# One pool of eight PSUM banks, the second part of batch 0 masked on VectorE, another order of the loads, and new instruction lists, in a fused attention and channel-mix kernel

## The chip, the cores and the metric

The kernel runs on one core of a Trainium2 chip. The metric is the device time in microseconds (us) of one execution. The five engines of the core work side by side, each in the order of its own instruction stream: TensorE (PE in the profile, with its weight loads listed apart as PEld), VectorE (DVE), ScalarE (ACT), GpSimd (POOL) and SyncE (SP). Here POOL issues the loads, SP the stores and the transposing DMAs.

## What is computed

Sliding-window attention with an ALiBi bias over 8 batches, 8 heads, 576 positions and a head dimension of 64; its output, regrouped to rows of 512, goes through an RWKV channel mix.

```python
scores = scale * np.matmul(q, k.transpose(0, 1, 3, 2))
bias = slopes[:, None, None] * (-np.abs(rel).astype(np.float32))[None, :, :]
mask = (rel >= 0) & (rel < window)            # window = 128
scores = np.where(mask, scores + bias[None], -1000000000.0)
attn = softmax(scores);  x = regroup(attn @ v)
...
xk = mu_k * x + (1.0 - mu_k) * x_prev         # x_prev: x one row earlier
xr = mu_r * x + (1.0 - mu_r) * x_prev
k = np.maximum(xk @ w_k, 0.0)
v = k * k @ w_v
return (1.0 / (1.0 + np.exp(-(xr @ w_r))) * v)
```

## The kernel before

**Tiles.** The 576 rows of a batch are four blocks of 128 and a tail of 64. Heads go in pairs, four groups `g` per batch. Since the window is 128, a query block meets its own key block and the one before. The scores of a group are computed in two halves, keys on the partitions, queries along the free dimension.

**Attention, batch by batch.** q and k are loaded with the sequence on the partitions (`cb`) and have to be transposed to `qk` (head dimension on the partitions). For batch 0, in two parts, PE transposes staged blocks (L1123, L1126, L1078); for batches 1 and 2 PE does it in quarters of 64 by 64 (L1078), for 3 and 4 in halves (L837), with copies out by ScalarE and VectorE (L696); for 5 to 7 (`XB`) SP issues transposing DMAs (`flip`, L535). The 64-row tails of q and k (`ts`) become `tt`: batch 0 by matmuls with parts of the identity (L939), batches 1 to 3 by PE transposes (L912), the rest (`XTT`) by a transposing DMA (L628). Then follow the score matmuls (L726), exp on ScalarE (L740) into `at`, and the matmuls with v and a column of ones (L781), which give output and row sum; VectorE takes the reciprocal (L787) and multiplies (L793) into `xu`. `xu` is transposed to `xt` (L820, L837, or by DMA, L902); VectorE forms the difference with the previous row (L880) and `xk` and `xr` (L887).

**Bias and mask.** In batch 0 PE first writes the ALiBi distance times the slope into the PSUM banks of the scores (L713: `sid` holds scaled identities, `dist` the distances), the score matmuls accumulate on it, and exp gives the finished weights. In the other batches exp runs on the bare scores, and VectorE multiplies with `mask`, the exp of the bias (L753). ScalarE makes `mask` from `dist` in eight activations (L1165), gated behind the last `xk` of batch 0's first part, and VectorE copies it to the other columns (L1191).

**Channel mix**, in chunks of 256, 384 or 512 rows (`channel_mix`): per chunk eight groups of four matmuls with `wk` (L983), ReLU on ScalarE (L990), the square on VectorE or ScalarE (L964, L962) into `kk`; then per 128 rows four matmuls with `wr` (L1001) and tanh (L1008), eight with `wv` (L1017) in two halves, and the product (L1022) to `ot`, which SP stores (L1047).

**Order.** The program builds a graph of nodes (`op`, `dma`). `Plan.run` is a planner: it walks the graph with estimated durations and gives every node its buffers (`Hold`). For PE, ACT and DVE the order is not the planner's choice but a table, `ORDER`: each list holds node numbers, and an engine takes the next of its list only. The planner's durations therefore decide the buffer numbers and the place of the DMAs. 90 small matmuls on a zero tile (`NWARM`, L687) are spread at the start.

**PSUM.** Eight banks of 512 floats: `duo0` and `duo1` are tiles of two banks for scores and the attention output of a whole group, `uno0` to `uno3` tiles of one bank for all else. The framework makes the waits from the tiles that instructions share.

**Loads.** POOL issues them in a fixed order, each only after the eighth before it has landed. For the start the string `LOADS` gives it, a letter for a step: `v` two blocks of v, `2` the second part of q and k of batch 0, `K` and `k` the halves of `wk`, `t` the tail of batch 0, `V` the rest of v, `a`, `b`, `c` q and k, tails, and v of batch 1, `R` all of `wr`, `W` and `w` the halves of `wv`.

Of the kernel before, what the change touches and what calls it, by code (L numbers as in the profile page):

```python
# [38 lines left out]
""".split()],  # L39
    "ACT": [int(x) for x in """  # L40
# [11 lines left out]
""".split()],  # L52
    "DVE": [int(x) for x in """
# [25 lines left out]
class Node:  # L79
    def __init__(self, seq, engs, dur, lat, prio, emit, need, free):  # L80
        self.seq, self.engs, self.dur, self.lat = seq, engs, dur, lat
        self.prio, self.emit, self.need, self.free = prio, emit, need, free
        self.left, self.succ = 0, []
        self.ready, self.t0, self.eng, self.queue = 0.0, None, None, None
        self.rows, self.lazy, self.flip = (128, 128), False, False


class Plan:
# [3 lines left out]
    SWITCH = 0.095  # L92
    CROSS = (0.45, 1.1)
# [67 lines left out]
    def run(self):  # L161
# [16 lines left out]
        while events:  # L178
# [11 lines left out]
            while again:  # L190
                again = False
                for e, cand in avail.items():
# [23 lines left out]
                    if e == "PE":  # L216
                        if n.rows[0] != rows:
                            n.dur = dur = dur + self.SWITCH
                        rows = n.rows[1]
                    busy[e] = now + dur  # L220
# [16 lines left out]
        return order  # L237


@with_exitstack  # L240
def kernel(
# [32 lines left out]
    XB = range(5, B)  # L274
    XO = range(5, B)
    X0 = 16
    NWARM = 90
    LOADS = 'v2KtVkabRWwc'
# [8 lines left out]
    QUAD = 0.040  # L287
# [86 lines left out]
    def one(h):  # L374
        return uno[h.idx if h.cls == "p1" else N1 + h.idx]

# [951 lines left out]
```

## Time and profile before

| what | us |
|---|---|
| median of 3 runs | 229.64 |
| lowest and highest run | 228.93 and 230.03 |
| span of the profiled execution | 228.6 |
| PE busy, fillers included | 222.9 |
| DVE busy | 189.2 |
| ACT busy | 156.3 |

The profiled execution's own time is known as its span only; it lies 1.0 us below the median and 0.3 below the lowest run. A busy PE is one with at least one matmul under way, and a matmul's row lasts from its start until its result is written, so that rows of neighbouring matmuls overlap: a matmul's price is the step from its start to the next one's. In the names the number of a buffer is left out. The loads run in one queue, in the order of their issue.

### The profile page before, as it was taken

How to read it: one execution, taken by the hardware profiler on the slowest of the kernel's cores; microseconds unless marked ns; L12 is line 12 of the kernel's file. 1: busy time of each engine (PE TensorE's matmuls, PEld its weight loads, DVE VectorE, ACT ScalarE, POOL GpSimd, SP SyncE). 2: the span in 40 equal slices, each digit the busy share in tenths (PEclk: the TensorE clock that was granted, in tenths of full speed). 3: DMA queues.
4: the chain of work that ended last, by engine and by line, in shares of the span. 5: the costliest groups of instructions: out<-in, count | busy, mean ns of one | idle time of the engine just before them, and what ended most of it. 6: DMA issues, size and time to landing. Idle time of an engine off the chain costs nothing.

```text
span 228.6 us, 6467 instructions
## 1 busy us (share of the span) xinstructions
PE 222.9 (97%) x2611; PEld 134.7 (59%) x2611; DVE 189.2 (83%) x423; ACT 156.3 (68%) x283; POOL 92.0 (40%) x118
## 2 busy tenths in 40 slices
PE   8998999999999999999999999999999999999994
PEld 8674866765667665456675654546755645465542
DVE  6788899999949998989899977899799889956332
ACT  2578899899999987998488735764788137336221
POOL 8755746698963980975029904200000000000000
PEclk9999999999999999999999999999999999999999
DMA  6999999999996999999999997994420461121123
GB/s 162 179 185 199 198 192 179 186 193 173 181 154 119 136 178 187 133 129 155 200 205 136 179 169 179 177 182 160 60 76 3 103 191 53 29 93 49 40 97 138
DMA packets 127741, 32.80 MB, mean 143 GB/s; under 512 B 114904, under 2 KB 123360, under 8 KB 127712
## 3 DMA queue, kind: packets, MB, share of 16 engines
q0 software_dynamic: 95728, 16.26, 93.7%
q1 hardware_dynamic: 30240, 15.54, 30.9%
q10 hardware_dynamic: 1744, 0.59, 1.1%
q8 instruction: 20, 0.33, 0.6%
q14 instruction: 9, 0.07, 0.1%
HBM read 33.56 MB, written 9.44 MB: 188 GB/s over the span
## 4 chain that ended last, share of the span: by engine, by line
PE 82%; DMA 10%; DVE 3%; POOL 1%; ACT 1%; issue 1%; DVEq 0%; POOLq 0%
PE uno L983 27%; PE uno L1017 25%; PE uno L1001 13%; PE duo L781 7%; PE duo L726 6%; DMA wk_sb<-in_moe_w_k_dram 5%; DMA qx<-in_q_dram 3%; DMA out_dram<-ot 2%; PE uno L837 2%; PE uno L1078 1%; POOL vs L500 1%; ACT at L740 1%; DVE ot L1022 1%; DVE xu L793 1%; PE uno L781 1%
## 5 line engine op out<-in xcount | busy, mean ns | idle before, releaser
L983 PE MATMUL uno<-xk,wk_sb 128*128 128x256 bf16 (+2 forms) x416 | 71.4, 314 | 1.1 <-DMA wk_sb<-in_moe_w_k_dram 0.9
L740 ACT ACTIVATE at<-duo 128x1024 bf16<-128x1024 f32 (+2 forms) x68 | 65.0, 989 | 10.6 <-PE duo L726 10.2
L1017 PE MATMUL uno<-wv_sb,kk 128*128 128x512 bf16 (+2 forms) x296 | 69.8, 374 | 0.0
L990 ACT ACTIVATE rl<-uno 128x256 bf16<-128x256 f32 (+2 forms) x104 | 46.6, 475 | 33.2 <-PE uno L983 26.1
L983 PEld LDWEIGHTS <-wk_sb 128*128 128x128 bf16 x416 | 38.9, 98 | 25.5 <-DMA wk_sb<-in_moe_w_k_dram 1.1
L1017 PEld LDWEIGHTS <-kk 128*128 128x128 bf16 x296 | 27.1, 98 | 27.8
L500 POOL DMA_DIRECT2D vs<-in_v_dram x32 | 28.4, 897 | 36.8 <-PE duo L781 33.6
L753 DVE TENSOR_TENSOR at<-at,mask 128x1024 bf16<-128x1024 bf16 x56 | 37.0, 684 | 5.7 <-ACT at L740 5.5
L964 DVE TENSOR_TENSOR kk<-rl 128x256 bf16<-128x256 bf16 (+2 forms) x94 | 30.0, 337 | 9.0 <-ACT rl L990 8.4
L1001 PE MATMUL uno<-wr_sb,xr 128*128 128x512 bf16 x144 | 36.4, 379 | 0.0
L1008 ACT ACTIVATE rs<-uno 128x512 bf16<-128x512 f32 x36 | 21.4, 610 | 16.9 <-PE uno L1001 13.6
L1022 DVE SCALAR_TENSOR_TENSOR ot<-rs,uno 128x512 f32<-128x512 bf16 (+2 forms) x37 | 24.4, 667 | 9.9 <-PE uno L1017 3.6
L887 DVE SCALAR_TENSOR_TENSOR xr<-dl,mu_sb,xt 128x576 bf16<-128x576 bf16 (+1 forms) x32 | 24.6, 777 | 0.0
L887 DVE SCALAR_TENSOR_TENSOR xk<-dl,mu_sb,xt 128x576 bf16<-128x576 bf16 (+1 forms) x32 | 24.4, 776 | 0.1
L781 PEld LDWEIGHTS <-at 128*128 128x128 bf16 x576 | 21.1, 97 | 5.0 <-issue 0.7
L793 DVE TENSOR_TENSOR xu<-duo,rc 128x640 bf16<-128x640 f32 x28 | 22.5, 813 | 0.2
L1001 PEld LDWEIGHTS <-xr 128*128 128x128 bf16 x144 | 13.2, 98 | 13.1 <-issue 0.2
L696 ACT COPY qk<-uno 128x512 bf16<-128x512 bf16 (+1 forms) x32 | 16.9, 582 | 3.2 <-PE uno L1126 2.5
L781 PE MATMUL duo<-vs,at 128*128 128x65 bf16 x448 | 18.7, 193 | 0.2
L531 POOL DMA_DIRECT2D cb<-in_k_dram x20 | 17.8, 924 | 2.1 <-DMA vs<-in_v_dram 1.6
L531 POOL DMA_DIRECT2D cb<-in_q_dram x20 | 17.7, 927 | 0.7 <-PE duo L781 0.6
L696 ACT COPY xt<-uno 128x512 bf16<-128x512 bf16 (+3 forms) x24 | 13.1, 567 | 1.7 <-PE uno L837 0.9
(82 smaller groups left out, 202.3 us busy)
## 6 DMA issues: line engine op xcount, KB each, us to landing
out_dram<-ot SPq DMA_DIRECT2D x34, 256.0 KB, 2.6
vs<-in_v_dram POOLq DMA_DIRECT2D x32, 128.0 KB, 6.8
cb<-in_q_dram POOLq DMA_DIRECT2D x20, 128.0 KB, 6.2
cb<-in_k_dram POOLq DMA_DIRECT2D x20, 128.0 KB, 6.7
wk_sb<-in_moe_w_k_dram POOLq DMA_DIRECT2D x2, 512.0 KB, 10.0
cb<-in_q_dram POOLq DMA_DIRECT2D x4, 256.0 KB, 9.7
cb<-in_k_dram POOLq DMA_DIRECT2D x4, 256.0 KB, 8.8
wv_sb<-in_moe_w_v_dram POOLq DMA_DIRECT2D x2, 512.0 KB, 11.4
```

What stands on the lines that cost most here:

```text
L500: return dma(POOL, 256, issue_t(1024), lambda e: nc.gpsimd.dma_start(out=vs_buf[h.idx][:, j, :, 0:D], in_=v[b, :, 128 * j:128 * j + 128].r ...
L531: return [dma(POOL, 256, issue_t(1024), lambda e, r=r: nc.gpsimd.dma_start(out=cb_buf[h.idx][:, i, r], in_=src[:, :, r]), [g], kind="q") f ...
L696: (nc.scalar.copy if e == ACT else nc.vector.tensor_copy)(out=out, in_=in_)
L740: lambda e, ah=ah, w=w, hp=hp: nc.scalar.activation(out=ah(), in_=two(hp)[:, :, 0:w], func=AF.Exp, scale=float(scale)), (), [hp])
L753: nc.vector.tensor_tensor(out=a, in0=a, in1=m, op=ALU.mult)
L781: nc.tensor.matmul(a[:, hl, t - t0], lhsT=at[:, lo:lo + 128], rhs=vs[:, u, 2 * g + hl, 0:W] if u < NF else tvb[:, 2 * g + hl, 0:W], start= ...
L887: lambda e: nc.vector.scalar_tensor_tensor(out=buf[hk.idx][:, g, e0 + c0:e0 + c1], in0=dls(), scalar=mu[:, g:g + 1], in1=xc(1), op0=ALU.mu ...
L964: nc.vector.tensor_tensor(out=out, in0=in_, in1=in_, op=ALU.mult)
L983: nc.tensor.matmul(one(hp)[:, 0:n], lhsT=wk_sb[:, po, 128 * fo:128 * fo + 128], rhs=xk_buf[hx.idx][:, po, c0:c1], start=(po == 0), stop=(p ...
L990: a = op(ACT, act_t(n), [s], pr, lambda e, hp=hp, hr=hr: nc.scalar.activation(out=rl_buf[hr.idx][:, 0:n], in_=one(hp)[:, 0:n], func=AF.Rel ...
L1001: nc.tensor.matmul(one(hp), lhsT=xr_buf[hx.idx][:, po, 128 * c:128 * c + 128], rhs=wr_sb[:, po], start=(po == 0), stop=(po == NPO - 1))
L1017: nc.tensor.matmul(one(hv)[:, a:b], lhsT=kk_buf[hk.idx][:, fo, o:o + 128], rhs=wv_sb[:, fo, a:b], start=(fo == 0), stop=(fo == NFO - 1))
```

## The change

1. **PSUM.** One tile `ps` of eight banks takes the place of the six. A node holds one bank or an aligned pair. A new class `Watch` records who last wrote and read each bank, adds a dependency where an instruction of another engine touches the same bank, and takes away those that the framework would add because all share one tile.
2. **Batch 0's second part** has no bias matmuls any more (`BM`); its two halves are multiplied with `mask` on VectorE like the other batches, the first of them in two instructions. In the first part the bias matmuls become a node of their own. `mask` is made early, without its gate: PE writes the biases of four heads into two banks in four matmuls, twice (`mask_pe`, L1197), and ScalarE takes the exp of each in one activation (L1202).
3. **Batch 0's tail** goes through 32 matmuls on quarters of 64 rows (`TQ`, L1015) in place of 16 on 128 rows, and four copies in place of two.
4. **Batch 4's q and k** (`XB`) and **batch 3's tail** (`XTT`) are transposed by DMA in place of PE.
5. **The two score halves** of a group are nodes of their own in batches 1 to 7 (`SS`).
6. **Order:** `LOADS` changes, `NWARM` goes from 90 to 56, the planner's costs change, and all three lists are new.

```diff
-    XB = range(5, B)
+    XB = range(4, B)
-    NWARM = 90
-    LOADS = 'v2KtVkabRWwc'
+    NWARM = 56
+    LOADS = 'v2tKVkRabWwc'
-    SS = ()
+    SS = range(1, B)
-    XTT = range(4, B)
-    MMASK = False
+    XTT = range(3, B)
+    MMASK = True
-    duo = [pst.tile([128, 2, 512], FP32, name=f"duo{i}") for i in range(2)]
-    uno = [pst.tile([128, 512], FP32, name=f"uno{i}") for i in range(4)]
+    NB = 8
+    ps = pst.tile([128, NB, 512], FP32, name="ps")
+    watch = Watch(tc, ps, NB)
...
+        if eng == "PE":
+            for b in set().union(*(self.banks(a) for a in outs)):
+                keep += self.readers[b]
+                self.readers[b] = []
+                self.writer[b] = (inst, eng)
+        else:
+            for b in set().union(*(self.banks(a) for a in ins if a.tensor.name == self.name)):
+                keep.append(self.writer[b])
+                self.readers[b].append((inst, eng))
+        keep = [n for n, e in keep if e != eng]
+        for n in keep:
+            self.tc.add_manual_dep(inst, n.name, SYNC, reason="bank")
...
+                if m0 == 512:
+                    nc.vector.tensor_tensor(out=ah(), in0=ah(), in1=m[:, :, 256:512], op=ALU.mult)
+                    return
+                if m0 == 128:
+                    for lo, n, c in ((0, 128, 128), (128, 256, 0)):
+                        nc.vector.tensor_tensor(out=ah()[:, :, lo:lo + n], in0=ah()[:, :, lo:lo + n],
+                                                in1=m[:, :, c:c + n], op=ALU.mult)
+                    return
...
-                s, (x,) = scores(0, g, [(pieces, m0, htt if uses_tt else None)], True, hq0[g], ha,
+                s, (x,) = scores(0, g, [(pieces, m0, htt if uses_tt else None)], m0 not in BM, hq0[g], ha,
```

POOL at the start, from the first load after the second part of batch 0's q and k (`ts_67` and `ts_68` are the tails of batches 0 and 1, `cb_61` the q and k of batch 1). Before:

```order
L541 DMA wk_sb<-in_moe_w_k_dram 128x4x512
L515 DMA ts_67<-in_q_dram 128x1x256
L515 DMA ts_67<-in_k_dram 128x1x256
L500 DMA vs_63<-in_v_dram 128x8x64 x2
L505 DMA tv_65<-in_v_dram 64x8x64
L541 DMA wk_sb<-in_moe_w_k_dram 128x4x512
L496 DMA cb_61<-in_q_dram 128x4x256
L496 DMA cb_61<-in_k_dram 128x4x256
L496 DMA cb_61<-in_q_dram 128x4x256
L496 DMA cb_61<-in_k_dram 128x4x256
L521 DMA ts_68<-in_q_dram 64x8x64
L521 DMA ts_68<-in_k_dram 64x8x64
```

The next row is the load of `wr`. POOL at the same place now:

```order
L578 DMA ts_67<-in_q_dram 128x1x256
L578 DMA ts_67<-in_k_dram 128x1x256
L604 DMA wk_sb<-in_moe_w_k_dram 128x4x512
L563 DMA vs_63<-in_v_dram 128x8x64 x2
L568 DMA tv_65<-in_v_dram 64x8x64
L604 DMA wk_sb<-in_moe_w_k_dram 128x4x512
L604 DMA wr_sb<-in_moe_w_r_dram 128x4x512
L559 DMA cb_61<-in_q_dram 128x4x256
L559 DMA cb_61<-in_k_dram 128x4x256
L559 DMA cb_61<-in_q_dram 128x4x256
L559 DMA cb_61<-in_k_dram 128x4x256
L584 DMA ts_68<-in_q_dram 64x8x64
```

The tail of batch 0 has moved ahead of the first half of `wk`, and `wr` ahead of batch 1; the loads of `wv` follow in both.

PE where it takes up the second half of `wk` (`DMASW` in brackets is a wait for a load, `Activation` one for ScalarE). Before, this is the second group of `wk` matmuls:

```order
L726 MATMUL duo_123<-qk_73 128x256
L983 LDWEIGHTS wk_sb [waits DMASW2_49]
L983 MATMUL uno_125<-xk_93,wk_sb 128x256 [waits Activation_49]
L983 LDWEIGHTS wk_sb
L983 MATMUL uno_125<-xk_93,wk_sb 128x256
```

Now it is the fourth:

```order
L1078 MATMUL ps<-xk_93,wk_sb 128x256
L1078 LDWEIGHTS wk_sb [waits DMASW2_49,Activation_49]
L1078 MATMUL ps<-xk_93,wk_sb 128x256
L1078 LDWEIGHTS wk_sb
L1078 MATMUL ps<-xk_93,wk_sb 128x256
```

Two groups of `wk` matmuls have moved ahead of the wait, and the wait for a free bank has moved from the matmul to the weight load. Over the whole program 309 weight loads wait for VectorE or ScalarE now, 76 before.

VectorE between the first part's `xk` and the second part's attention output. Before:

```order
L887 SCALAR_TENSOR_TENSOR xr_95<-ot_111,mu_sb,xt_89 128x256
L696 COPY qk_73<-uno_127 128x2x128
L887 SCALAR_TENSOR_TENSOR xr_95<-ot_111,mu_sb,xt_89 128x256 x2
L787 RECIPROCAL rc_81<-uno_127 128x2x3
L964 TENSOR_TENSOR kk_100<-rl_97 128x256
L793 TENSOR_TENSOR xu_85<-uno_127,rc_81 128x2x3x64
```

Now:

```order
L961 SCALAR_TENSOR_TENSOR xk_93<-ot_111,mu_sb,xt_89 128x256 x2
L819 TENSOR_TENSOR at_77<-at_77,mask 128x2x128
L819 TENSOR_TENSOR at_77<-at_77,mask 128x2x256
L961 SCALAR_TENSOR_TENSOR xr_95<-ot_111,mu_sb,xt_89 128x256
L819 TENSOR_TENSOR at_79<-at_79,mask 128x2x128
L819 TENSOR_TENSOR at_79<-at_79,mask 128x2x256
L815 TENSOR_TENSOR at_77<-at_77,mask 128x2x256
L815 TENSOR_TENSOR at_79<-at_79,mask 128x2x256
```

Twelve multiplications with `mask` have come in ahead of the second part's reciprocals, the last two after the first of them.

More of the change, by code (lines that the diff above doesn't have):

```diff
@@ L219, in run @@
                         rows = n.rows[1]
+                        if now < self.COLD:
+                            n.dur = dur = dur * n.cold
                     busy[e] = now + dur
@@ L394 @@
     NBIAS = 4
+    BM = (128, 512)
+    TQ = True
     XRL = 4.0
@@ L703, in scores, with emit_bias @@
             w = sum(n for _, _, n in pieces)
-            todo.append((pieces, m0, tt, a0, w, Hold("p2")))
+            todo.append((pieces, m0, tt, a0, w, Hold("p1", 2)))
             dur += sum(max(n / 2400 + .0025, .03) for _, _, n in pieces)
-            dur += 0.01 + (2 * mm(w) if bias else 0)
+        def emit_bias(e):
+            for (pieces, m0, tt, a0, w, hp) in todo:
+                for hl in range(2):
+                    nc.tensor.matmul(
+                        two(hp)[:, hl, 0:w], lhsT=sid[:, 2 * g + hl], rhs=dist[:, m0:m0 + w],
+                        start=True, stop=False, skip_group_check=True)
         def emit(e):
             qk = qk_buf[hq.idx] if hq.cls == "qk" else qx_buf[hq.idx][:, :, g]
-            if bias:
-                for (pieces, m0, tt, a0, w, hp) in todo:
-                    for hl in range(2):
-                        nc.tensor.matmul(
-                            two(hp)[:, hl, 0:w], lhsT=sid[:, 2 * g + hl], rhs=dist[:, m0:m0 + w],
-                            start=True, stop=False, skip_group_check=True)
             for (pieces, m0, tt, a0, w, hp) in todo:
@@ L727, in emit @@
                                          start=not bias, stop=True, skip_group_check=True)
-        if b == 0 and parts[0][1] == 0 and g < 2:
-            dur *= 1.6
-        s = op(PE, (0.12 if bias else 0.02) + dur, deps, prio + (2,), emit, list(need) + [x[5] for x in todo], free)
-        s.rows = (128 if bias else 64, 64)
+        hps = [x[5] for x in todo]
+        if bias:
+            s = op(PE, sum(2 * mm(x[4]) for x in todo) + 0.03, [n_dist] + list(n_copy.values()) +
+                   n_sid[2 * g:2 * g + 2], prio + (2,), emit_bias, hps)
+            deps, hps = list(deps) + [(s, 0.0)], []
+        s = op(PE, 0.03 + dur, deps, prio + (2,), emit, list(need) + hps, free)
+        s.rows = (64, 64)
         res = []
@@ L933, in tails, with emit_q @@
             return tails_full(b, prio, htt, hs)
+        if TQ:
+            hp = [Hold("p1"), Hold("p1")]
+            def emit_q(e):
+                for n in range(8):
+                    for hl, r in ((0, 0), (1, 1), (1, 0), (0, 1)):
+                        rows = slice(64 * r, 64 * r + 64)
+                        nc.tensor.matmul(
+                            one(hp[r])[64 * hl:64 * hl + 64, 32 * n:32 * n + 32],
+                            lhsT=ts_buf[hs.idx][rows, n],
+                            rhs=ident[rows, rows].rearrange("p (c g t) -> p t g c", g=G, t=2)[:, hl],
+                            start=n == 0, stop=True, skip_group_check=True)
+            t = op(PE, 0.28, list(tl[b]) + [n_ident], prio + (0,), emit_q, hp, [hs])
+            t.rows = (65, 65)
+            g = virtual("tt", [htt])
+            c = [op(DVE, dve_t(128), [t, g], prio + (0,), lambda e, i=i, r=r: copy_any(
+                e, tt_buf[htt.idx][:, :, i, 32 * r:32 * r + 32].rearrange("p g (c r) -> p g c r", r=4),
+                one(hp[r])[:, 128 * i:128 * i + 128].rearrange("p (r g c) -> p g c r", r=4, g=G)),
+                    (), [hp[r]]) for i in range(2) for r in range(2)]
+            return htt, c
         hp = Hold("p1")
@@ L1091, in qk_quad, with make_mask, mask_pe, emit @@
         return hq, ys
+    def make_mask(h):
+        nc.scalar.activation(out=mask[:, h, 0:256], in_=dist[:, 0:256],
+                             func=AF.Exp, scale=-(2.0 ** (-(h + 1))))
+    def mask_pe(j):
+        hp = Hold("p1", 2)
+        def emit(e):
+            for h in range(4):
+                nc.tensor.matmul(two(hp)[:, h // 2, 256 * (h % 2):256 * (h % 2) + 256],
+                                 lhsT=sid[:, 4 * j + h], rhs=dist[:, 0:256],
+                                 start=True, stop=True, skip_group_check=True)
+        m = op(PE, 4 * mm(256), [n_dist] + n_sid[4 * j:4 * j + 4], (2, 2 * j), emit, [hp])
+        return op(ACT, act_t(1024), [m], (2, 2 * j + 1), lambda e: nc.scalar.activation(
+            out=mask[:, 4 * j:4 * j + 4, 0:256],
+            in_=two(hp).rearrange("p b (h c) -> p (b h) c", h=2), func=AF.Exp,
+            scale=float(scale)), (), [hp])
+    if MMASK:
+        ms = [mask_pe(j) for j in range(2)]
+    else:
+        ms = [op(ACT, act_t(256, True), [n_dist], (2, h), lambda e, h=h: make_mask(h))
+              for h in range(H)]
+    n_mcopy = []
+    for j, (c0, n) in enumerate(MSEG):
+        n_mcopy.append(op(DVE, dve_t(8 * n, 4), ms + n_mcopy, (2, j),
+                          lambda e, c0=c0, n=n: nc.vector.tensor_copy(
+            out=mask[:, 0:H, c0:c0 + n], in_=mask[:, 0:H, 0:n])))
+    n_mask = ms[-1]
     xks, xrs = {}, {}
@@ L1296 @@
             if n.emit is not None:
+                done = len(nc.cur_bb.bb.instructions)
                 n.emit(n.eng)
+                if n.eng in ORDER:
+                    for inst in nc.cur_bb.bb.instructions[done:]:
+                        watch.note(inst, n.eng)
 _INS = ['q', 'k', 'v', 'moe_mu_k', 'moe_mu_r', 'moe_w_k', 'moe_w_v', 'moe_w_r']
```

97 lines of the change are left out of this document (52 added, 45 removed), and 84 rows, old and new, of the table ORDER.

## Prediction

> **What bounds the kernel now.** I read the page first, then the chain of waits in order of time, then the busy time by stretches, and last the timeline of the two engines that matter, PE and POOL (which issues the loads).
>
> ```profile
> span 228.6 us, 6467 instructions
> PE 222.9 (97%) x2611; PEld 134.7 (59%) x2611; DVE 189.2 (83%) x423; ACT 156.3 (68%) x283; POOL 92.0 (40%) x118
> ```
>
> PE is busy for 97% of the span, but that holds the 90 filler matmuls too, so the page alone does not say where useful work begins. The chain does:
>
> ```profile
> 3.99 7.10 DMA qx<-in_q_dram
> 11.38 10.68 DMA wk_sb<-in_moe_w_k_dram
> 22.10 0.61 PE uno L983 x4
> ```
>
> Up to 22.1 us the chain is a queue of loads: q, then the second half of wk. From 22.10 it is almost all PE, up to the last matmuls, which the timeline shows:
>
> ```profile
> 224.13 1.26 PE L1017 MATMUL uno<-wv_sb,kk 128*128 128x384 bf16 x12
> 225.82 0.36 ACTq L1041 DMA_DIRECT2D out_dram<-ot  x1
> ```
>
> PE is done at 224.13 + 1.26 = 225.39; 3.2 us of output follow, which the change leaves as they are. So the end is "when the loads let PE go" plus "what PE still has to do then". The busy time by stretches (bounds and length, then busy us of PE, PEld, DVE, ACT and POOL, the granted clock, DMA) shows how much air the other engines have behind PE:
>
> ```profile
> 16.00:22.00 6.00, 5.20 (x98) 3.14 (x97) 5.28 (x16) 5.78 (x15) 3.76 (x6) 1.00 1.44 198
> 22.00:30.00 8.00, 7.90 (x166) 6.21 (x166) 6.65 (x21) 6.63 (x18) 5.69 (x7) 1.00 1.43 198
> 30.00:40.00 10.00, 9.93 (x171) 6.00 (x158) 9.29 (x21) 9.65 (x16) 5.26 (x8) 1.00 1.76 183
> 40.00:60.00 20.00, 19.88 (x364) 13.28 (x363) 19.42 (x38) 18.71 (x37) 17.56 (x21) 1.00 2.10 185
> 60.00:80.00 20.00, 20.00 (x312) 13.02 (x310) 16.13 (x35) 19.50 (x39) 14.40 (x19) 1.00 1.85 141
> ```
>
> From 30 to 80 us all three engines are nearly full. Each load is issued only when the eighth before it has landed, so POOL's waits (in brackets: idle us before the row, and what ended it) date the landings:
>
> ```profile
> 22.34 1.59 POOL L541 DMA_DIRECT2D wv_sb<-in_moe_w_v_dram  x2 [2.58 <-DMA wk_sb<-in_moe_w_k_dram]
> 24.50 0.89 POOL L500 DMA_DIRECT2D vs<-in_v_dram  x1 [0.57 <-DMA cb<-in_k_dram]
> 30.58 0.76 POOL L496 DMA_DIRECT2D cb<-in_q_dram  x1 [0.89 <-DMA wr_sb<-in_moe_w_r_dram]
> 33.13 0.74 POOL L496 DMA_DIRECT2D cb<-in_k_dram  x1 [1.79 <-DMA wv_sb<-in_moe_w_v_dram]
> ```
>
> The second half of wk is in by 22.3 (PE takes it at 22.10), batch 1's first k part by 24.5, wr by 30.58, the first half of wv by 33.13. One weight load takes 2.55 us of the queue (33.13 - 30.58).
>
> **The change part by part.** The prices on PE are steps from one start to the next in the chain:
>
> ```profile
> 23.79 0.33 PE duo L713 x2
> 24.85 0.22 PE duo L713 x2
> 26.80 0.87 PE uno L983 x8
> 29.55 0.22 PE uno L820 x3
> 34.60 0.86 PE uno L1001 x4
> 35.90 0.55 PE duo L726 x12
> 36.44 0.38 PE uno L1078 x32
> 41.05 1.10 PE duo L781 x36
> 63.45 0.22 PE uno L912 x4
> 63.67 0.57 PE uno L837 x32
> 69.96 0.48 PE uno L837 x32
> ```
>
> *PE work that goes.* Batch 0's second part loses its bias matmuls: 4 x (0.33 + 0.22) = 2.2 us. The mask comes back as 8 matmuls of 256 columns, 4 x 0.22 = 0.9 us, but before 10 us, where fillers run. Batch 4 loses 64 half transposes, 0.57 + 0.48 = 1.05 us by batch 3's rows, batch 3 its 4 tail transposes, 0.22 us; both lie past 60 us, where PE is full, so they count whole: 1.27 us. The batch 0 tail in quarters (16 matmuls of 128 rows to 32 of 64) lies before 20 us, where fillers still run: nothing. So do the 34 fillers dropped.
>
> *The loads.* wr moves from behind batch 1's q, k and tail to ahead of them; the tail of batch 0 moves ahead of wk's first half. The bytes ahead of wk's second half and ahead of wv are the same set, so these land at 22.1 and 33.15 as before. What moves is batch 1: its q and k land one weight load later, the first k part at 24.5 + 2.55 = 27.05.
>
> *PE against those landings.* In the new list PE waits for wk's second half at its fourth group of wk matmuls (before: at its second). From there to the first batch 1 transposes it has 20 wk matmuls (2.2 us), 48 attention matmuls (1.5) and 9 transposes (0.66): 4.3 us, so it is there at 26.4 and waits till 27.05. Then to the first wv matmul: one and a half blocks of transposes (0.57), 8 wr matmuls (1.72), 3 transposes (0.22), 8 score matmuls (0.37), two more blocks (0.76), the tail (0.22), 16 score matmuls (0.73): 4.6 us, 31.65, and wv lands only at 33.15. So PE waits 1.5 us there: this gate sets the gain.
>
> ```profile
> 33.56 1.04 PE L1017 MATMUL uno<-wv_sb,kk 128*128 128x512 bf16 x4
> ```
>
> Before, PE came to that matmul at 33.56 and needed 225.39 - 33.56 = 191.83 us from it. After, one more block of transposes lies behind it (0.38) and 1.27 us are gone: 190.18 us. PE ends at 33.15 + 190.18 = 223.33, that is 2.06 us earlier. So of some 3.3 us of useful work that leaves the stage past 22 us, about 1.2 is spent waiting for wv.
>
> *VectorE.* Four multiplies of 256 and eight of 512 elements come in. Neighbouring rows:
>
> ```profile
> L880 DVE TENSOR_TENSOR ot<-xt 128x256 bf16<-128x256 bf16 x4 | 1.0, 273 | 0.1
> L753 DVE TENSOR_TENSOR at<-at,mask 128x1024 bf16<-128x1024 bf16 x56 | 37.0, 684 | 5.7 <-ACT at L740 5.5
> L696 DVE COPY tt<-uno 128x512 bf16<-128x512 bf16 x3 | 1.3, 423 | 0.4 <-PE uno L912 0.4
> L696 ACT COPY qk<-uno 128x512 bf16<-128x512 bf16 (+1 forms) x32 | 16.9, 582 | 3.2 <-PE uno L1126 2.5
> ```
>
> 512 elements cost between 0.27 and 0.68; I take 0.45, so 4 x 0.27 + 8 x 0.45 = 4.7 us. ScalarE takes over three copies (some 0.42 each) and a cast (0.7): net +2.7 us. From 16 to 30 us VectorE had 2.1 us free, and PE's two waits cover as much again. I count nothing, with the rest as a rival. ScalarE loses eight copies of batch 4, 8 x 0.58 = 4.7 us, behind the stretch in which it is full: no gain of its own.
>
> *Transposing DMAs.* Nine more go through SP's queue, and outputs queue behind them there.
>
> ```profile
> 58.27 3.54 POOL L531 DMA_DIRECT2D cb<-in_q_dram  x4
> 88.44 11.49 SPq L535 DMA_TRANSPOSE qx<-cb  x7
> ```
>
> Batch 4's loads are issued from 58 us on; eight transposes at 11.49 / 7 = 1.6 us take 13 us, while PE has the scores of batches 2 and 3 ahead of batch 4's. The output buffers held meanwhile are two of five. I take nothing; if PE had to wait for the last two, 3 us.
>
> *The bank waits.* With one tile for all banks the wait for a free bank stands on the weight load, no longer on the matmul: 309 weight loads wait for another engine, 76 before. Of the old ones, this is the wv load that waits for VectorE:
>
> ```profile
> 211.81 0.60 PE L983 MATMUL uno<-xk,wk_sb 128*128 128x256 bf16 x4
> 212.14 0.64 PEld L1017 LDWEIGHTS <-kk 128*128 128x128 bf16 x4
> 212.25 1.03 PE L1017 MATMUL uno<-wv_sb,kk 128*128 128x512 bf16 x4
> ...
> L1017 PEld LDWEIGHTS <-kk 128*128 128x128 bf16 x296 | 27.1, 98 | 27.8
> ```
>
> The four matmuls before it take 4 x 0.109 = 0.44 us, 211.81 + 0.44 = 212.25: nothing is lost. I take 0; exposed, each costs its 98 ns, at most 23 us for 233 more. Beside this row: the Trainium skill, "TensorE: Matmul & The Clock Gate", Step-by-step, says that PE pulls weight loads ahead of running matmuls; by that rule a load that still waits cannot be pulled, and at the columns / 1.2 GHz that the section LDWEIGHTS gives, 107 ns each, 233 of them would add an estimated 25 us if all came late. The trace agrees that the pull survives a wait met in time; it shows no late bank.
>
> Sum: the profiled execution had 228.6 us, the median of the runs is 229.64; I carry the difference of 1.0 over. 228.6 - 2.1 = 226.5 in the profile, **227.5 us** as a median. (The measurement can tell 0.5%, 1.15 us, from no change.)
>
> **The rivals.** *No wait at the loads* (0.20). If batch 1 and wv land earlier than dated, the work alone decides: against the old list at 22.10 the new one lacks 8 wk matmuls (0.87), three pairs of bias (0.77), 16 score matmuls (0.73) and the 1.27, and has one attention more (0.37): 3.27 us, 226.4. For it: a landing can lie before the wait that dates it. Against: the same bytes.
>
> *VectorE sets the start* (0.17). If its 2.7 us push the masks of batch 0 and then, since it has only 1.3 us free from 30 to 60, batch 1's attention, PE loses its lead of 0.8 us (0.41 at wv, 0.38 for the block of transposes), only the 1.27 us past 60 are left (228.4), or it loses up to 1.1 more (229.5); I take 229.0. For it: DVE 19.42 of 20.
>
> *Late banks stall the weight loads: slower* (0.10). Price 0.1 us each where the freeing engine is not 0.1 us early. From 21 exposed loads the gain is gone, from 33 it is over 0.5% slower; a third of 233 gives 7.7 us less 2.1, 235. For it: ScalarE and VectorE, which free the banks, are full from 30 to 80 us. Against: the row at 212.14, and eight banks in one pool come free earlier than two pairs did.
>
> *The clock drops* (0.05).
>
> ```profile
> 0.99 5.42 PE L687 MATMUL uno<-warm 128*128 128x128 bf16 x51 [0.99 <-DVE warm L469]
> 12.08 0.50 PE L687 MATMUL uno<-warm 128*128 128x128 bf16 x6
> ```
>
> The granted clock reads 1.00 in every stretch, but the first 51 fillers take 106 ns each and six later ones at most 83: PE starts slow. The new list has no fillers after about 8 us. If it fell back to half speed, the 4.3 us after wk took 8.6, wv began at 35.3, and 2.15 us were lost: 229.6. The Trainium skill, "TensorE: Matmul & The Clock Gate", HAM clock gate, has such a fall after an idle window of about 3.4 us; no gap of that length is left in the list as I read it, and the trace's first rows agree with its slow start.
>
> **How the numbers follow.** Forecast 0.48, the rivals 0.20, 0.17, 0.10, 0.05. Faster: 0.48 + 0.20 + 0.04 of VectorE's case = 0.72; same: its other 0.13, the clock's 0.05 = 0.18; slower 0.10. The range goes from just under the work-only case to the clock's: 226.1 to 229.7; outside it lie the late banks and some of the edges.
>
> **What would show it.** Right: no bias matmuls in batch 0's second part; PE waiting for cb near 26.5 and for wv at about 32 to 33; PE's last matmul near 223.3; no transposes of cb in batch 4. Wrong: the first wv matmul before 32.5 or after 34; gaps of 0.1 us in front of most wk groups; DVE as the releaser of PE between 22 and 45 us; filler-length matmuls of twice the duration after 10 us.

## The result, and the profile after

The changed kernel takes 231.87 us (median of four runs, 230.63 to 233.3), the kernel before 229.28 beside it: a ratio of 1.0107, 95% interval 1.0059 to 1.0155. Seven more runs later gave 231.21 against 229.37, 1.0072 (1.0046 to 1.0098). So it is slower by some 0.7 to 1.1%; the forecast was 227.5, faster by 0.9%. Runs over 1.5% above the fastest of their kernel are left out of all medians and ratios here: one of run 2 (298.5 us, clock 0.709), two of run 4 (233.98 and 234.16, clock 0.978), one each of runs 8 and 11.

The profiled execution looks the other way at first. Its page:

```profile
span 228.2 us, 6317 instructions
PE 219.5 (96%) x2517; PEld 128.7 (56%) x2517; DVE 188.5 (83%) x431; ACT 153.3 (67%) x274; POOL 92.1 (40%) x118
PEclk9976999999999999999999999999999999999999
```

PE is busy 3.4 us less, and the span is 0.4 us shorter than the 228.6 of before. But this execution took 231.85 us, 3.65 more than its span: part of the loss lies outside what the profile calls the span. And the line of the granted clock, all nines before, has a 7 and a 6 in it.

The busy time by stretches of 2 us (bounds, length, then PE, PEld, DVE, ACT, POOL, granted clock, DMA) shows where the clock fell:

```profile
12.00:14.00 2.00, 1.74 (x90) 1.34 (x88) 1.46 (x9) 1.74 (x6) 1.33 (x2) 1.00 1.30 204
14.00:16.00 2.00, 1.46 (x42) 1.01 (x36) 2.00 (x8) 1.86 (x8) 0.99 (x3) 0.68 2.24 165
16.00:18.00 2.00, 1.60 (x26) 0.89 (x21) 2.00 (x9) 2.00 (x4) 1.01 (x2) 0.50 1.48 198
18.00:20.00 2.00, 1.73 (x8) 1.04 (x8) 2.00 (x8) 1.96 (x5) 1.75 (x3) 0.50 1.24 207
20.00:22.00 2.00, 2.00 (x20) 1.48 (x20) 1.47 (x5) 1.16 (x2) 0.77 (x1) 0.62 1.30 201
```

PE has idle time from 12 to 20 us, VectorE none from 14 to 20 (2.00 of 2), and the clock is at a half from 14.70 to 21.53 us. The fall comes 0.7 us after VectorE fills up; from 12 to 14 us VectorE is busy 1.46. In the kernel before PE was busy 1.99, 2.00, 2.00 and 2.00 us in the first four of these stretches, at 1.00. PE's own rows (timeline) show what a half means, and that the first wv matmul comes on the forecast time all the same:

```profile
18.27 1.89 PE L1078 MATMUL ps<-xk,wk_sb 128*128 128x256 bf16 x8 [0.31 <-ACT at L806]
22.36 1.03 PE L1078 MATMUL ps<-xk,wk_sb 128*128 128x256 bf16 x8
33.12 1.90 PE L1112 MATMUL ps<-wv_sb,kk 128*128 128x512 bf16 x8
49.89 0.39 PE L789 MATMUL ps<-qk 64*128 64x256 bf16 x3 [0.50 <-ACT xt L759]
73.49 0.63 PE L855 MATMUL ps<-vs,at 128*128 128x65 bf16 x15 [0.60 <-ACT qk L759]
223.62 1.26 PE L1112 MATMUL ps<-wv_sb,kk 128*128 128x384 bf16 x12
```

Eight wk matmuls take 1.89 us at 18.27 and 1.03 at 22.36. The first wv matmul starts at 33.12 (forecast 33.15), but PE ends at 223.62 + 1.26 = 224.88, not at 223.33: 1.55 us are lost behind that point. Two of the places are in the list: PE waits for a bank that a copy of ScalarE (xt, qk) has yet to read. In the kernel before PE waits for no such copy past 33 us.

### The profile page after: what moved, and what is told of

Read it like the earlier page. It is cut to its first block, busy times and chain, and to the rows that moved or that the text cites. A ratio compares the mean times of both kernels' runs of the same rounds, so it can differ in the third digit from the quotient of the medians.

```text
span 228.2 us, 6317 instructions
## 1 busy us (share of the span) xinstructions
PE 219.5 (96%) x2517; PEld 128.7 (56%) x2517; DVE 188.5 (83%) x431; ACT 153.3 (67%) x274; POOL 92.1 (40%) x118
## 4 chain that ended last, share of the span: by engine, by line
PE 85%; ACT 7%; DMA 3%; POOL 2%; issue 1%; DVE 0%; DVEq 0%; POOLq 0%; ACTq 0%
PE ps L1078 28%; PE ps L1112 26%; PE ps L1096 14%; PE ps L855 7%; PE ps L789 7%; DMA qx<-in_k_dram 3%; ACT qk L759 3%; ACT at L806 2%; PE ps L911 1%; ACT xt L759 1%; ACT rl L1085 1%; POOL vs L563 1%; PE ps L1173 1%; POOL qx L559 0%; PE ps L1015 0%
## 5 line engine op out<-in xcount | busy, mean ns | idle before, releaser
L1078 PE MATMUL ps<-xk,wk_sb 128*128 128x256 bf16 (+2 forms) x416 | 72.6, 318 | 0.3 <-ACT at L806 0.3
L1085 ACT ACTIVATE rl<-ps 128x256 bf16<-128x256 f32 (+2 forms) x104 | 46.9, 475 | 38.4 <-PE ps L1078 30.9
L1112 PE MATMUL ps<-wv_sb,kk 128*128 128x512 bf16 (+2 forms) x296 | 70.1, 374 | 0.0
L806 ACT ACTIVATE at<-ps 128x1024 bf16<-128x1024 f32 (+2 forms) x68 | 63.4, 987 | 5.0 <-PE ps L789 4.0
L1112 PEld LDWEIGHTS <-kk 128*128 128x128 bf16 x296 | 26.6, 98 | 29.7 <-ACT rs L1103 1.0
L1096 PE MATMUL ps<-wr_sb,xr 128*128 128x512 bf16 x144 | 36.4, 380 | 0.0
L1103 ACT ACTIVATE rs<-ps 128x512 bf16<-128x512 f32 x36 | 21.6, 612 | 21.7 <-PE ps L1096 21.7
L1117 DVE SCALAR_TENSOR_TENSOR ot<-rs,ps 128x512 f32<-128x512 bf16 (+2 forms) x37 | 24.2, 660 | 10.3 <-PE ps L1112 10.2
L867 DVE TENSOR_TENSOR xu<-ps,rc 128x640 bf16<-128x640 f32 (+2 forms) x36 | 26.5, 742 | 0.3
L855 PE MATMUL ps<-vs,at 128*128 128x65 bf16 x512 | 22.1, 193 | 0.6 <-ACT qk L759 0.6
L1096 PEld LDWEIGHTS <-xr 128*128 128x128 bf16 x144 | 13.0, 98 | 14.2 <-ACT rl L1085 0.7
L759 ACT COPY qk<-ps 128x512 bf16<-128x512 bf16 (+1 forms) x27 | 13.6, 552 | 2.6 <-PE ps L1252 2.2
```

Source lines behind the costliest of these rows:

```text
L806: lambda e, ah=ah, w=w, hp=hp: nc.scalar.activation(out=ah(), in_=two(hp)[:, :, 0:w], func=AF.Exp, scale=float(scale)), (), [hp])
L855: nc.tensor.matmul(a[:, hl, t - t0], lhsT=at[:, lo:lo + 128], rhs=vs[:, u, 2 * g + hl, 0:W] if u < NF else tvb[:, 2 * g + hl, 0:W], start= ...
L867: nc.vector.tensor_tensor(out=out_, in0=a5()[:, :, :, 0:D], in1=rc[:, :, 0:nt, None].to_broadcast([128, 2, nt, D]), op=ALU.mult)
L1078: nc.tensor.matmul(one(hp)[:, 0:n], lhsT=wk_sb[:, po, 128 * fo:128 * fo + 128], rhs=xk_buf[hx.idx][:, po, c0:c1], start=(po == 0), stop=(p ...
L1085: a = op(ACT, act_t(n), [s], pr, lambda e, hp=hp, hr=hr: nc.scalar.activation(out=rl_buf[hr.idx][:, 0:n], in_=one(hp)[:, 0:n], func=AF.Rel ...
L1096: nc.tensor.matmul(one(hp), lhsT=xr_buf[hx.idx][:, po, 128 * c:128 * c + 128], rhs=wr_sb[:, po], start=(po == 0), stop=(po == NPO - 1))
```

## The experiments

Every run has its time, its span and its mean granted clock; a window of 3.41 us at half clock lowers that mean by 3.41 / 2 / 228 = 0.0075. "Excess" is the time less the span. Runs are numbered as their expectations stand here by label: e12 is run 12. Spans are given as medians, clocks as ranges.

**The time outside the span.** First the kernel before, unchanged.

> The kernel before, unchanged, to have the time, the span and the granted clock of its runs side by side: of the changed kernel's four runs the time lies 1.8 to 3.7 us above the span (231.85 with 228.2, 230.63 with 228.7). If that part belongs to the run and not to the program, the kernel before shows 1.8 to 3.7 us too, with spans of about 226 to 227.5 and a clock of 1.00. If it belongs to the changed program, the kernel before shows 0.2 to 1.4 us, with spans of about 228.6.

Twelve runs: 229.59 us, excess 1.72 to 1.84, spans 227.4 to 228.9 (median 227.8), clock 0.998 to 1.00. In 93 more runs of the kernel before, on four chips, the median span was 227.6 to 227.7. So the excess of 1.8 belongs to every program here, and what lies above it to the changed one; the 228.6 of its profile was one of its longer runs. The changed kernel again, and with 40 matmuls behind its end:

> The changed kernel, unchanged, twelve runs with span and clock. In the kernel before, and in the runs with fillers, the time lies 1.75 to 1.8 us above the span in every run. In the trace of the changed kernel two fetches of instructions (16 KB and 8 KB) start at 230.4 and 230.5 us and end at 232.1, behind the last instruction of the span (228.2). Theory of the late fetch: part of the runs lie 1.8 us above their span, part 2.5 to 3.8, and the mean of the excess over 1.8 is about 1 us. Against it: an excess that goes with the span or the clock. Median 231 to 232; spans 228 to 230, longer where the clock is lower.

> The changed kernel with 40 more matmuls on the zero tile behind its last one: PE runs them while the last output is under way, and nothing waits for them. They move the place in PE's instruction stream at which its last 16 KB are asked for to well ahead of the end. Theory of the late fetch: the time is 1.8 us above the span in all runs, spans as in the run without, the median 0.8 to 1.3 us lower: 230.3 to 231. If the fetch is harmless: same median within 0.4 us.

```python
+                if final and a and f1 == NFO:          # behind the last wv matmul
+                    for _ in range(40):
+                        nc.tensor.matmul(ps[:, (hv.idx + 4) % 8, 0:128], lhsT=warm, rhs=warm, ...)
```

Unchanged: excess 1.79, 1.81, 1.90, 1.93, 1.95, 3.03 and 3.43. With the 40 matmuls: 1.73 to 1.82 in all twelve runs. The trace's DMA records show the cause. One queue, which the page lists as "instruction", fetches 16 KB at a time, on average once per 253 records of PE (65 bytes each), so it is taken for PE's instructions:

```
kernel                        its last two fetches at   last instruction
before, first run above       185.8   206.8             227.8 us
changed, first profile        199.8   230.5 to 232.1    228.2
changed, second profile       199.5   230.2             227.9
changed, 40 matmuls more      202.8   225.7             231.3
```

The changed program is some 170 PE instructions shorter, and its 20th fetch falls due right at its end: in both traces it starts 2.3 us behind the last instruction. Its end (232.1 and 231.2 us) goes with the time of these two runs (231.85 and 230.93), some 0.3 us behind it in both. The eleven runs of the changed kernel range from 1.79 to 3.65, with a mean of 2.41: 0.6 us more than before. In run 7 further down, where the 20th fetch comes at 221.7 us, the excess is 1.74 to 1.86 in all six runs without the 40 matmuls. The median did not fall as expected (231.12), since in these twelve runs the clock was lower than ever (0.978 to 0.993, spans 227.9 to 231.3, median 229.35). That is the other part.

**The clock.** More fillers in the changed kernel, and fewer in the kernel before:

> The changed kernel with 52 small matmuls on the zero tile put into the nodes of batch 0 between about 9 and 20 us (0.056 us each at the full clock, 2.9 us in all, most of it where PE stands idle). Clock theory: the granted clock stays at 1.00, the score and wk matmuls between 15 and 21.5 us run at full rate, and the stall of about 3 us that grew between 10 and 22 us goes; PE is then held by the loads, so 1 to 2.5 us are gained: 229.4 to 230.9. Theory of the waits on weight loads: no gain, 231.5 to 232.5, though the clock is back. Theory of the lists (ScalarE behind PE from 26 us on): the clock is back, the gain is under 0.7 us, since ScalarE and VectorE are full from 30 to 45 us anyway: 231.2 to 232.

```python
+    def pad(bank, n): ...   # n matmuls on the zero tile, into the bank that the node writes next
+            pad(two(todo[0][5])[:, 0], 2)    # scores of the second part; 3 each ahead of the first
+                                             # part's attention and transposes, and of the quads
```

> The kernel before without its 32 fillers after 10.6 us, the mirror of the second run. Clock theory: the granted clock falls to a half for about 7 us between 12 and 24 us, and the kernel is 1 to 3 us slower: 230.3 to 232.3. Other theories: PE is not the bound there, since it waits for wk until 22.1 us: 228.8 to 229.8, whatever the clock does.

```python
     def emit_warm(e):
+        n_put[0] += 1
+        if n_put[0] > 58:
+            return
```

The 52 fillers hold the clock (0.997 to 1.00), and the kernel takes 230.96, spans 228.8 to 229.7: no long runs, but none of the short ones either. They cost about what the clock gives. The mirror holds: the kernel before, without 32 fillers, falls to half clock (15.25 to 22.08 us in its trace; 0.984 to 1.00 over ten runs) and takes 230.8, ratio 1.0056 (1.0030 to 1.0082). Then only 28 fillers, between 9 and 16 us, and with them the next edit:

> The changed kernel with the 40 matmuls behind its end and 28 fillers in batch 0 between about 9 and 16 us (3 ahead of each attention node of the first part, 4 ahead of each block of transposes of the second). Clock theory: clock 1.00 in all runs, spans of 227.9 to 228.5 without the long ones of 229 to 231 that the run with the 40 matmuls alone had; median 229.8 to 230.2. If the fillers cost what the clock gives, as the 52 did (spans 228.8 to 229.7): 230.6 to 231.

> As the run with 28 fillers and the 40 matmuls, and the bank waits on the matmul in place of the weight load. Theory that a bank wait on a weight load costs something: spans 0.4 to 0.6 us shorter than there, 227.2 to 227.9 (the runs of that change alone with the clock at 1.00 had 227.0 to 227.8, the changed kernel at that clock 227.9 to 228.2); median 229.0 to 229.6. Theory that it is free: same as there within 0.2 us.

Both expectations fell: 232.36 and 232.00 us, clock 0.985 to 0.993 in every run. The stretches of the first of them show why:

```profile
14.00:16.00 2.00, 2.00 (x82) 1.56 (x79) 1.16 (x8) 1.20 (x4) 1.01 (x2) 1.00 2.23 162
16.00:18.00 2.00, 1.52 (x47) 0.90 (x35) 2.00 (x8) 1.61 (x6) 1.75 (x3) 1.00 1.46 203
18.00:20.00 2.00, 1.04 (x22) 0.63 (x21) 2.00 (x9) 2.00 (x4) 0.79 (x2) 0.88 1.24 206
20.00:22.00 2.00, 1.69 (x12) 1.04 (x8) 1.73 (x6) 2.00 (x5) 0.76 (x1) 0.50 1.30 201
```

The fillers close PE's gaps up to 16 us, delay the work behind them, and leave the gap from 16 to 20 us. The clock falls later, at 19.50, and stays low to 26.33, over the wk matmuls.

What a stretch has to hold is not PE's busy time. The clock changes in steps of 3.41 us (last section), so the traces can be cut into windows of that length. Count the matmuls of each by their share of the array and their columns, as parts of a filler (128*128 of the array, 128 columns): a row of 64*64 and 64 columns counts an eighth. The windows that end at the twelve falls in the traces (run 8's left out) hold 15.0 to 22.5 fillers' worth; of the 932 other windows at full clock one holds 22.1 and the rest 23.1 or more. PE's busy time does not part them: 1.92 to 2.81 us of 3.41 ahead of a fall, the longest gap 0.23 to 1.32 us, but 2.09 us with a gap of 1.40 in a window of run 7 (from 27.86) that no fall follows. This was read off the traces afterwards; no run was made to test it.

**The bank waits.** In the changed kernel the added dependencies put the wait for a bank on the weight load. Without them the framework's own remain, and put it on the matmul:

> The changed kernel with the framework's own bank dependencies in place of the added ones: the waits for VectorE and ScalarE then stand on 266 matmuls and 72 weight loads, against 16 and 322 in the changed kernel. Theory of the waits on weight loads: the stalls of 0.1 to 0.8 us ahead of scores and wk groups between 26 and 80 us shrink, 1 to 3 us gained: 229 to 231. Clock theory and theory of the lists: no change beyond 0.3 us, 231.5 to 232.2, clock 0.985 as before.

```python
-        for n in keep:
-            self.tc.add_manual_dep(inst, n.name, SYNC, reason="bank")
```

> As the second of these runs without its fillers: the price of the clock alone, with the late fetch gone. Clock theory: part of the runs at 0.976 to 0.99 with spans of 228.5 to 230, the others at 1.00 with 227.0 to 227.8, median 0.5 to 1.5 us above the run with fillers. If the fall costs nothing because PE waits for loads and for ScalarE until 33 us anyway: spans the same whatever the clock.

229.96 us (excess 1.76 to 3.77, so with late fetches among them), and with the 40 matmuls 229.77, ratio 1.0024 (0.9999 to 1.0049; excess 1.73 to 1.87). The two together give a table of span by clock, and the price of a window:

| clock (windows at half) | spans of these 24 runs |
|---|---|
| 1.00 (none) | 227.0 to 227.9, mean of twelve 227.47 |
| 0.99 to 0.993 (one) | 227.7 to 229.0 |
| 0.985 (two) | 228.9 to 229.6 |
| 0.976 (three) | 230.0 |

Each window costs some 0.85 us. (In runs 5 and 6, with the wait on the weight load, one window cost nothing, 228.1 against 228.0, and two 1.3 us, 229.3.) The changed kernel at 1.00 had 227.9, 228.0 and 228.2, three runs only; so the place of the wait is worth about 0.55 us. Runs 9 and 10 differ in it alone: at a clock of 0.985 their mean spans are 230.8 and 230.5, so there it is 0.3. The stalls that I blamed on it stay, row for row, on the matmul (timeline of PE, run 12):

```profile
50.06 0.38 PE L788 MATMUL ps<-qk 64*128 64x256 bf16 x3 [0.51 <-ACT xt L758]
74.00 0.62 PE L854 MATMUL ps<-vs,at 128*128 128x65 bf16 x15 [0.57 <-ACT qk L758]
```

**What sits behind the stalls past 30 us.** ScalarE's load, or the choice of the bank:

> The changed kernel with the exp of batches 1 to 3 on half of its columns (the other half is left out; the buffers are filled with ones at the start): 24 activations of 1024 elements, 0.99 us each, become 24 of 512, about 0.55 us, so ScalarE loses some 10 us of work between 30 and 75 us. Theory of ScalarE as the bound: PE's stalls between 30 and 80 us go from about 3.7 us to under 1, and the span is 2 to 3 us shorter: 225.5 to 227. Theory of the choice of banks or of any fixed cost: under 0.7 us shorter.

```python
-                out=ah(), in_=two(hp)[:, :, 0:w], func=AF.Exp, ...
+                out=ah()[:, :, 0:w // 2] if b in (1, 2, 3) else ah(),
+                in_=two(hp)[:, :, 0:w // 2 if b in (1, 2, 3) else w], func=AF.Exp, ...
```

> The changed kernel with another choice of the bank: of the free ones that which came free first (singles still from broken pairs first). Theory that PE's stalls from 30 to 75 us come from the choice of the banks (it is given a bank that the planner takes for free, and whose reader is late): the stalls at about 30.3, 31.1, 31.6, 48.9, 54, 61.5 and 71.9 us (3.9 us together) shrink by half or more, the span by 1 to 2 us. Theory that ScalarE's work is what PE waits for there, whichever the bank: stalls and span unchanged within 0.4 us.

```python
-        return max(free, key=lambda a: ((a ^ 1) not in free, a))
+        return max(free, key=lambda a: ((a ^ 1) not in free, -self.when.get(a, 0)))   # pairs likewise
```

The first took 237.66 us: filling the buffers with ones held VectorE up, PE stood idle for 5.73 us up to 11.38, the first wv matmul came 7.2 us late, and the total says nothing. Its stalls do: with half the exp work they measure 0.68, 0.58, 0.37 and 0.75 us where the changed kernel has 0.71, 0.54, 0.34 and 0.77 at the same four places (step between rows less the matmuls' own price). Its trace ran at a clock of 0.95 between the falls, so this speaks against ScalarE's total load as what PE waits for, and does not rule it out. The second took 231.33, spans 229.2 to 230.3: the stalls at 54, 61.5 and 72 us are gone, a new one of 1.63 us stands at 29.7. With that choice from 38 us on only:

> As the run before, and from 38 us of the planner's time on the bank that came free first. Theory that PE's stalls from 46 to 75 us come from the choice of the bank: those at about 54, 61.5 and 72 us (1.6 us) go, as they went when that choice was made from the start, without the new stall of 1.63 us at 29.7 that it brought there; span 1 to 1.5 us shorter, 226.0 to 226.8. Theory that later stages take it back (the older choice had 0.6 us more stall past 100 us): under 0.5 us.

232.45 us, against 232.00 without. Again one stall went (at 72) and another grew, to 1.70 us at 50.8; one of 1.12 at 105.7 is new. Another bank moves the stalls; it does not remove them.

**The list, and VectorE's masks.** Two neighbours swapped in PE's list, so that wv matmuls which need no new bank go ahead of a node that waits for one; and, apart from it, the bias back on PE. Both start from run 12's kernel (40 matmuls more, bank waits on the matmul):

> Same base, two neighbours swapped in PE's list twice: near 48.9 us the second wv half ahead of the scores that wait for a bank, near 71.9 us the second wv half ahead of the attention that waits for a bank. Theory of the order (PE has other work ready, and the list holds it back): stalls of 0.72 and 0.95 us go, spans 1.2 to 1.6 us shorter, 225.8 to 226.6 at clock 1.00. Theory that ScalarE or VectorE is late anyway: the stalls come back elsewhere before 90 us, under 0.5 us shorter.

```
-  357 456 489 296 290      +  357 456 296 489 290     (489: scores, 296: second wv half)
-  402 450 403 434          +  402 403 450 434         (450: attention, 403: second wv half)
```

> Base: the changed kernel with the 40 matmuls behind its end and the bank waits on the matmul (run 12: spans 227.2 to 227.9 at clock 1.00, 228.1 to 229.6 below). Edit: the bias of batch 0's second part goes back to PE (16 matmuls of 384 or 256 columns, 2.2 us), its 12 multiplies on VectorE (4.7 us) are gone; the early mask stays for the other batches. Theory that VectorE's masks starve PE between 14 and 20 us and so let the clock fall: PE busy again in 14 to 20 us, clock 1.00 in nearly all runs, spans 226.5 to 227.5, median 228.3 to 229.3, below the kernel before. Theory of the fillers alone (too few, whatever VectorE does): the clock still falls in half of the runs, spans 227.5 to 230.

```python
+            if b == 0 and not bias:
+                emit_bias(e)                       # ahead of the score matmuls
-                                         start=not bias, stop=True, ...
+                                         start=not bias and b > 0, stop=True, ...
+                if b == 0:                         # in the node of the multiply
+                    return
```

> Both edits on the same base. If both theories hold: clock 1.00, spans 225.3 to 226.3, median 227.1 to 228.1, faster than both kernels. If only one holds: as the better of the two alone.

The swaps: 228.40 us, ratio 0.9949 (0.9932 to 0.9966), faster than both kernels. Five of these six runs had the clock at 1.00, against half of run 12's; in so few that may be luck, and it lowers the median. Spans at clock 1.00 are free of it: 226.2 to 226.9, 0.9 us under run 12's. PE's rows at the two places, without a wait now:

```profile
49.67 0.38 PE L790 MATMUL ps<-qk 64*128 64x256 bf16 x4
49.98 1.04 PE L1113 MATMUL ps<-wv_sb,kk 128*128 128x512 bf16 x4
50.95 0.28 PE L790 MATMUL ps<-qk 64*128 64x256 bf16 x2
...
72.12 1.89 PE L1113 MATMUL ps<-wv_sb,kk 128*128 128x512 bf16 x7
73.85 0.62 PE L856 MATMUL ps<-vs,at 128*128 128x65 bf16 x15
```

The bias back on PE: 230.38 us, and the clock is at 1.00 in ten runs of twelve (run 12: six, the changed kernel: three of eleven). The stretches, of this kernel and then of run 12:

```profile
14.00:16.00 2.00, 1.47 (x66) 1.24 (x66) 1.89 (x11) 1.86 (x8) 0.91 (x2) 1.00 2.12 167
16.00:18.00 2.00, 1.87 (x16) 0.60 (x17) 2.00 (x9) 1.73 (x5) 1.75 (x3) 1.00 1.54 196
18.00:20.00 2.00, 2.00 (x31) 1.04 (x31) 1.13 (x3) 1.72 (x4) 0.90 (x2) 1.00 1.25 208
```

```profile
14.00:16.00 2.00, 1.34 (x68) 1.11 (x61) 1.75 (x9) 1.86 (x8) 1.44 (x2) 1.00 2.13 166
16.00:18.00 2.00, 1.18 (x26) 0.81 (x27) 2.00 (x8) 2.00 (x5) 1.13 (x2) 1.00 1.55 194
18.00:20.00 2.00, 1.54 (x13) 1.07 (x13) 2.00 (x8) 2.00 (x5) 1.73 (x3) 0.53 1.24 208
```

With the bias PE is busy 1.87 and 2.00 us from 16 to 20; with the masks 1.18 and 1.54, while VectorE is full, and the clock falls. The edit does two things, though: it relieves VectorE, and it gives PE work. PE's rows with the bias:

```profile
16.13 0.48 PE L772 MATMUL ps<-dist,sid 128*128 128x384 bf16 x2 [0.20 <-DVE qk L758]
16.55 0.34 PE L790 MATMUL ps<-qk 64*128 64x128 bf16 x4
16.82 0.50 PE L772 MATMUL ps<-dist,sid 128*128 128x384 bf16 x2
```

Twelve of the sixteen bias matmuls lie between 16 and 20 us and take 2.26 us (steps), more than the 1.15 us by which PE's busy time rose. Without them the emptiest 3.41 us of this trace would hold 11 fillers' worth, with them 18. So they do themselves what fillers did; that VectorE's relief held the clock, as the expectation had it, is not shown.

At 1.00 the bias costs a microsecond: spans of 227.9 to 229.1, mean 228.4, against 227.47. So the masks gain 0.95 of the 2.2 us that they were to gain, and the clock takes it back in the runs in which it falls. Both edits together: 229.62, ratio 1.0009 (0.9983 to 1.0036), not the 227.1 to 228.1 expected; at 1.00 their mean span is 227.6, 0.8 under run 13's, so the swaps gain nearly the same a second time.

## Why the prediction was wrong

Measured from the median span of the kernel before (227.7), the forecast's 2.06 us give 225.6, and with the excess of 1.8 a time of 227.4. The eleven runs of the changed kernel have a mean of 231.29 (span 228.88, excess 2.41). The 3.9 us between, by the runs:

| what | us | from |
|---|---|---|
| instruction fetch past the end | 0.6 | mean excess 2.41 against 1.78 |
| half clock after 14 us | 0.85 | mean span 228.88 against 228.03 at 1.00 |
| bank wait on the weight load | 0.55 | 228.03 against 227.47 |
| two places of the list | 0.9 | 227.47 against 226.54 |
| not traced to a run | 0.9 | 226.54 against the forecast's 225.6 |

*The fillers dropped: nothing.* This step failed first. It looked at whether PE had to wait anyway, and not at what the fillers did besides: 32 fewer cost the kernel before 1.3 us (run 4). The rival on the clock named the mechanism and gave it 0.05; its reason against was that no gap of 3.4 us is left in the list. No gap that long is needed: in the 3.41 us ahead of the falls PE was busy 1.92 to 2.81 us, with no gap over 1.32. In the trace of run 1 the emptiest 3.41 us past 8 us hold 30 fillers' worth, 15 if its fillers are not counted and 17 if the second part's bias matmuls are not; in run 5's trace, ahead of the fall, 17. The price of 2.15 us was of the right order for the worst runs (three windows, 2.5 us).

*VectorE's net +2.7 us: nothing.* VectorE did not move the first wv matmul (33.12), as the rival on VectorE had it. It fills 14 to 20 us, and PE idles there. Whether this idling brings the clock down is open: in the first profile, and in the traces of runs 3, 6, 14 and 15, the clock fell at 14.2 to 15.9 us, and in run 15 without the masks.

*The loads and the gate.* Right in its date, wv at 33.12 for 33.15, by luck: the cause was another. The landings came about a microsecond earlier than dated (the wait that dates the first half of wv ends at 32.27), so it was ScalarE's releases that PE waited for ahead of it:

```profile
32.27 0.74 POOL L559 DMA_DIRECT2D cb<-in_k_dram  x1 [0.62 <-DMA wv_sb<-in_moe_w_v_dram]
32.48 0.34 PE L789 MATMUL ps<-qk 64*128 64x256 bf16 x4 [0.49 <-ACT at L806]
```

*From the gate 190.18 us.* Failed: 191.76 in both traces of the changed kernel, as good as the 191.83 and 192.10 of the kernel before. The step took the old stage, subtracted work, and so supposed that the new list runs as dense as the old one. It does not: bank waits from 46 to 75 us that the old list hadn't. That PE ends 1.55 us late in this trace is this term alone; the half clock before 22 us was made up by 33 us there (in run 5's trace, with one low window in place of two, the first wv matmul came at 32.88). Where the clock stays low to 24.4 us or longer it is not: 34.86, 35.85 and 36.54 in the traces of runs 3, 6 and 9.

*The bias matmuls, 2.2 us less.* Right in kind; at full clock putting them back costs 0.95 us net of VectorE's relief.

*The bank waits: 0.* Mis-sized, 0.55 us by three runs against twelve (0.3 by runs 9 and 10). The rival's 7.7 us were far off: most of these waits end in time.

*The difference of 1.0 us carried over.* It is 1.72 to 1.85 in every run of the kernel before; the profiled run was long by as much as that was short, so the base of 229.6 stood. That a program's length could add to it was not in the sum.

*No cb transposes in batch 4; the tail of 3.2 us.* As forecast: 228.18 less 224.88 leaves 3.3.

Open stays the last 0.9 us. Most of it lies behind the first wv matmul (190.94 us with the swaps, for 190.18): the waits ahead of wv and several of 0.2 to 0.4 us from 40 to 90 us are in the trace of the swapped list too, and were not taken apart.

## What to carry to other kernels

Work taken off TensorE is worth its price only while the clock holds: before fillers or large matmuls go, count what is left in each stretch by its share of the array, not by PE's busy time. When a list is rebuilt, the old list's density can't be carried over; read where a node waits for a bank while work that needs none stands behind it. And compare the time with the span over several runs before explaining a difference inside the profile.

## What the runs showed of the hardware

- The granted clock changes only in steps of 3.41 us: in the traces full stretches last, among others, 10.24, 13.65, 208.21, 221.87 and 225.28 us, low ones 3.41, 6.83 and 10.24. The first full one begins at 3.9 to 6.9 us, differently in each run, which fits that one and the same program falls in some runs and not in others. The Trainium skill, "TensorE: Matmul & The Clock Gate", in its part on the HAM clock gate, has a free-running window of 3413 ns, and the traces agree. The same part of the Trainium skill gives the fall after an idle window of that length; here PE was partly busy throughout, which is nearer to the same page's second failure mode, psum-queue depth-cycling, where short idle times between groups of matmuls suffice.
- What went with a fall here was the array's work in a window: 15.0 to 22.5 fillers' worth (128 x 128 x 128) ahead of the twelve falls, 23.1 or more in all but one of 932 windows without one. At full clock a filler's step is 0.056 us, so 61 fit, and the border lies near 37% of that. Low windows that were followed by another low one held 16.8 to 25.0, those after which the clock came back 25.0 to 32.1.
- Fillers help the windows that they lie in: 28 of them up to 16 us left the next window short, and the clock fell at 18.2 to 19.5 us in the three traces and was low in all 17 runs (9 to 11); 52, some of them past 16 us, held it.
- Instructions are fetched in 16 KB pieces while the program runs, and a piece that falls due at the very end is waited for: up to 2.0 us outside the span, gone with 40 matmuls more.
- Some 250 bank waits moved from the weight load to the matmul took 0.3 to 0.55 us off the span here, all together.
